# First units' values by whole rows and a GpSimd spread, a new instruction list, and the zero products moved to the front

## The chip, the cores and the metric

The kernel runs on 1 core of a Trainium2 chip. The metric is the device time of one execution in microseconds. The kernel before was timed three times: median 895.59 us (895.14 to 896.82). A further execution was recorded by the hardware profiler.

## What is computed

Attention over q, k, v of shape (8, 8, 576, 64) in float32, followed by a feed-forward stage on the 4608 x 512 result:

```python
scores = 1/sqrt(D) * q @ k^T
mask_plain = (rel >= 0) & (rel < 32)                      # heads 0 to 3
mask_dil   = (rel >= 0) & (rel < 128) & (rel % 4 == 0)    # heads 4 to 7
attn = softmax(where(mask, scores, -1e9))
x = (attn @ v) laid out as (B*S, 512)
h = x @ w_in                                              # 512 x 2048, float64 weights
g = h * tanh(log1p(exp(min(h, 20))))                      # mish
out = g @ w_out                                           # 2048 x 512, float64 weights
```

The weights arrive as 64-bit floats. The host only lays arrays out and back (q and k transposed, dilated heads sorted by residue, the result transposed).

## The kernel before

**Units.** The work is cut into 16 units, a unit being half of one batch entry's sequence (288 tokens). For a unit, `loads` (step ld) fetches q and k, `loads_v` (lv) the values, `scores_of_pair` (sp), `scores` (sc) and `exps` (ex) form the windowed scores and their exponentials, `transpose_p` (tp), `values` (va) and `transpose_x` (tx) give the attention output with features on the partitions, and `ff1` (ff), `gate` (gt) and `ff2` (fo) or, from unit 8 on, `product` (fq) do the feed-forward stage. Step names carry the unit and the head pair: va1.2 is unit 1, pair 2. A step is a Python generator; each time its name stands in the list, it issues its next part.

**Units 0 to 2** are "direct": their scores and values are float32 matmuls without splitting into two halves, and values have a 65th column of ones per head, so that the value product also gives the softmax denominator. `prep` (pr) finds the largest magnitude of a unit's values; the denominators' step on ScalarE (L829) needs the scale that comes out of it.

**Weights.** w_in (4 groups of 512 columns, two halves each, steps 0.g.p) and w_out (1.g.p) come as 64-bit words through four buffers of 1 MB (`w_load`, wl). Each half goes through `w_max` (wm, ScalarE L400 for w_in, GpSimd L398 for w_out), `w_words` (ww: GpSimd L441, then VectorE L443 and L445), a maximum over the group on TensorE and VectorE (`w_scale`, ws: L412 or L415, L419) and `w_split` (wp: ScalarE L452, VectorE L454) into two float16 parts. A buffer is free again after its L454.

**The order** is written out: `ORDER` is a list of some 2250 step names, and every engine and queue executes its instructions in the order in which the list issues them. A queue never overtakes: an instruction that waits holds up all behind it on its engine. SyncE's queue carries every load and store. `=n` behind a name picks a PSUM bank.

**Zero products.** `keep_warm` (kw, L1137 to 1140) issues n matmuls of a zero tile, 128 columns wide, into a PSUM bank; nobody reads them. The list holds 42 ahead of the first scores (kw16, kw16, kw10) and 101 more between unit 0's and unit 2's attention (kw9, kw16, kw16, kw8, kw10; kw8; kw16, kw16; kw2).

**Values of a direct unit** (L494 to L510) are loaded straight into the tile with 65 columns per head, so each row of 1 KB in memory becomes four pieces of 256 B; a unit takes three such transfers for the plain heads (L508) and four for the dilated ones (L510).

## Time and profile before

| | us |
|---|---|
| median of three runs | 895.59 |
| the profiled execution | 897.61 |
| its span, first to last instruction | 895.6 |
| PE (TensorE matmuls) busy | 875.9 (98%) |
| DVE (VectorE) busy | 706.0 (79%) |
| ACT (ScalarE) busy | 621.4 (69%) |
| POOL (GpSimd) busy | 69.9 (8%) |

Times in the rows further down are counted from the span's start. PEld is TensorE's weight load, which overlaps matmuls. SPq is SyncE's DMA issue. The granted clock of TensorE is given as a share of 2.4 GHz: 0.50 is 1.2 GHz. A DMA share is the mean busy share of the core's 16 DMA engines. In brackets behind an instruction stands how long its engine had been idle before it and what ended that.

### The profile page before, as it was taken

To read this page: it belongs to the slowest core of one execution; us is meant where nothing else is said; L and a number is where in the kernel's file an instruction comes from. 1 tells how busy PE (TensorE), PEld (TensorE's weight loads), DVE (VectorE), ACT (ScalarE), POOL (GpSimd) and SP (SyncE) were. 2 spreads that over 40 slices of the span, in tenths; PEclk is the share of its full clock that TensorE was granted. 3 is DMA by queue.
4 is the path that set the end of the run, shared out by engine and by line. 5 is a ranking of instruction groups with operands and counts; after the bars stand their busy time and mean duration, and the time that the engine had idled before them with its cause. 6 is when DMAs were issued, how large, how long until landed. Compare 5 with 4: busy or idle time off the path is not lost.

```text
span 895.6 us, 23819 instructions
## 1 busy us (share of the span) xinstructions
PE 875.9 (98%) x10264; PEld 741.2 (83%) x10266; DVE 706.0 (79%) x1035; ACT 621.4 (69%) x924; POOL 69.9 (8%) x117
## 2 busy tenths in 40 slices
...
PEclk9699999999999999999999999999999999999999
...
GB/s 211 186 272 199 108 142 10 105 29 160 68 106 72 103 87 70 104 149 47 136 102 83 69 47 133 74 113 74 115 69 42 131 79 50 43 35 72 15 28 28
DMA packets 161464, 84.34 MB, mean 94 GB/s; under 512 B 127056, under 2 KB 157264, under 8 KB 161360
## 3 DMA queue, kind: packets, MB, share of 16 engines
...
## 4 chain that ended last, share of the span: by engine, by line
PE 90%; DVE 3%; DMA 2%; POOL 1%; SPq 1%; ACT 1%; issue 1%; DVEq 0%; ACTq 0%; POOLq 0%
PE b L923 39%; PE b L1111 21%; PE b L1062 18%; PE b L672 4%; PE b L821 4%; PE b L815 1%; DVE w L443 1%; POOL w L398 1%; DMA raw<-in_w_out 1%; DMA vn<-in_v 1%; DVE raw L445 1%; DVE w L454 1%; PE b L415 1%; DMA x<-x 0%; PE b L792 0%
## 5 line engine op out<-in xcount | busy, mean ns | idle before, releaser
L923 PE MATMUL b<-x,w 128*128 128x288 f16 x3072 | 390.0, 286 | 1.4 <-ACT den L829 1.1
L923 PEld LDWEIGHTS <-w 128*128 128x128 f16 x3072 | 297.8, 98 | 75.7 <-DVE w L454 1.2
L1111 PE MATMUL b<-g,w 128*128 128x288 f16 x1536 | 198.6, 286 | 0.0
L1111 PEld LDWEIGHTS <-w 128*128 128x128 f16 x1536 | 147.3, 98 | 36.9 <-issue 0.2
L929 ACT ACTIVATE hm<-b,fs 128x576 f32<-128x576 f32 x128 | 92.9, 737 | 73.2 <-PE b L923 68.6
L1062 PE MATMUL b<-g,w 128*128 128x144 f16 x1536 | 101.2, 226 | 0.4 <-DVE y L1081 0.2
L1062 PEld LDWEIGHTS <-w 128*128 128x128 f16 x1536 | 97.6, 98 | 1.6 <-issue 0.6
L1034 ACT ACTIVATE g<-hm,sg 128x1152 f16<-128x1152 f32 (+1 forms) x64 | 71.5, 1127 | 16.9 <-PE b L1062 14.0
L1036 DVE SCALAR_TENSOR_TENSOR g<-hm,sg,g 128x1152 f16<-128x1152 f32 (+1 forms) x64 | 79.8, 1261 | 4.3 <-ACT g L1034 4.2
L743 ACT ACTIVATE sb<-sb,ln_p 96x768 f32<-96x768 f32 (+3 forms) x52 | 46.1, 893 | 10.4 <-DVE sb L704 10.3
L704 DVE TENSOR_TENSOR sb<-sb,nm 96x512 f32<-96x512 f32 (+4 forms) x64 | 49.2, 769 | 2.2
L1081 DVE SCALAR_TENSOR_TENSOR y<-b,fo,y 128x144 f32<-128x144 f32 x48 | 20.6, 475 | 38.2 <-ACT y L1076 23.7
L782 DVE TENSOR_TENSOR p<-sb,p 96x768 f16<-96x768 f32 (+3 forms) x52 | 47.0, 905 | 4.5 <-ACT p L780 4.4
L702 DVE TENSOR_REDUCE nm<-sb 96x4 f32<-96x512 f32 (+4 forms) x64 | 48.8, 763 | 1.8
L1042 DVE TENSOR_TENSOR hm<-hm 128x576 f32<-128x576 f32 x64 | 47.8, 754 | 2.8 <-ACT hm L929 1.8
L1076 ACT ACTIVATE y<-b,fo 128x288 f32<-128x288 f32 x32 | 24.7, 779 | 34.5 <-PE b L1062 34.3
L1013 DVE SCALAR_TENSOR_TENSOR g<-hm,sg,g 128x1152 f16<-128x1152 f32 x32 | 44.8, 1409 | 2.8 <-ACT g L1011 2.8
L836 DVE TENSOR_TENSOR xs<-b,rec 96x384 f32<-96x384 f32 (+1 forms) x64 | 39.7, 621 | 5.8
L780 ACT CAST p<-sb 96x768 f16<-96x768 f32 (+3 forms) x52 | 40.8, 790 | 2.8 <-DMA pT<-p 2.6
L1011 ACT ACTIVATE g<-hm,sg 128x1152 f16<-128x1152 f32 x32 | 39.8, 1249 | 3.6 <-PE b L1111 3.2
L1062 PE MATMUL b<-g,g 128*128 128x144 f16 x576 | 40.3, 226 | 1.1 <-ACT y L1076 1.1
L821 PEld LDWEIGHTS <-pT 128*128 128x128 f16 (+2 forms) x1092 | 39.3, 98 | 1.7
(169 smaller groups left out, 1166.4 us busy)
## 6 DMA issues: line engine op xcount, KB each, us to landing
...
```

The lines of the kernel that those rows point to most:

```text
L702: nc.vector.tensor_reduce(nm[:nq, :, j:j + n], x, axis=AX.X, op=ALU.max, negate=True)
L704: nc.vector.tensor_tensor(blocked(sb, c0, n, w), x, nm[:nq, :, j:j + n].unsqueeze(3).broadcast_to([nq, 2, n, w]), op=ALU.add)
L743: nc.scalar.activation(x, x, AF.Exp, bias=ln_p[:nq])
L782: nc.vector.tensor_tensor(lo, src, hi, op=ALU.subtract)
L821: nc.tensor.matmul(avv[:, h, j], pp[:nk, c:c + P], vv[vi][:nk, j, hh, :], start=(i == 0), stop=(i == 2))
L923: nc.tensor.matmul(ph[:, h, :HT], w1[j][:, c, wi, k * P:(k + 1) * P], x_of(d, xi, c), start=(n == 0), stop=(n == len(seq) - 1))
L929: nc.scalar.activation(d["m"][p][:, half, k0:k0 + 2], ph[:, :, :HT], AF.Mish, scale=d["fs"][:, j:j + 1])
L1034: nc.scalar.activation(hi, src, AF.Identity, scale=sg)
L1036: nc.vector.scalar_tensor_tensor(lo, src, sg, hi, ALU.mult, ALU.subtract)
L1042: nc.vector.tensor_tensor(a, a, b, op=op)
L1062: nc.tensor.matmul(acc[e], left(l, e, p, wi)[:, k * P:(k + 1) * P], right(gi, k), start=(n in opens and p == 0 and q == 0), stop=(last and ...
L1111: nc.tensor.matmul(po[:, :HT], w2[:, e, j, wi, k * P:(k + 1) * P], d["g"][j][:, gi, k, :], start=(j == 0 and n == 0), stop=(j == NCH - 1 a ...
```

## The change

- `loads_v`: all plain blocks of a unit come in one transfer (two for the first half of a batch entry) and all dilated residues in one, by whole rows of 1 KB. For units 0 to 2 they land in a part of w_out's still empty tile `w2` (float32), and a second part of the step copies them with GpSimd into the tile with 65 columns per head. Unit 0's transfers are issued by ScalarE's queue, all others by SyncE's.
- `keep_warm` writes into a fixed strip of 96 columns of the last bank, 96 columns per product. The list holds 56 such products (kw32, kw24) ahead of the first scores and none later.
- `ORDER` is new as a whole. Unit 1's values are loaded before unit 0's and both ahead of the first weights; unit 2's values come before unit 2's q and k.
- `product` takes its three output slices from `po` where they exist; this only allows other orders of the steps.

The code, and of both lists the start (up to the second maximum of w_out) and the last lines:

```diff
@@ -26,6 +26,7 @@
 SPLIT_EXP = 13
 SUM_EXP = 14
 OUT_EXP = 12
+WIDE_MAX = 96
 LOW_SCALE, LOW_BIAS = 0.9375 * 2.0 ** -29, -2.0 ** -5
 TINY = 2.0 ** -40
 EXP_BITS = 0x7F800000
 ORDER = """
-mf cs3 ld0 cs1 xa0 xa1 cs0 kw16=0 kw16=0 kw10=0 sp0.0=0 sp0.1=1 sp0.2=2 lv0 pr0 sp0.3=3 sc0.1 ex0.1 wl0.0.0 lv1 ex0.1
-sc0.3 ex0.3 sc0.2 ex0.2 wl0.0.1 sc0.0 ex0.3 pr0 pr0=1 wl0.3.1 tp0.3=3 wl0.3.0 ld1 pr0 pr1 pr0 ex0.2 tp0.2=2 pr0 tp0.3
-wm0.0.0 ww0.0.0 ex0.0 va0.3=3 ww0.0.1 ww0.0.0 tp0.2 va0.2=1 ex0.0 tp0.0=2 va0.3 va0.2 va0.3 tp0.1=0 va0.2 ww0.3.1
-tx0.3=3 tp0.0 va0.0=2 tx0.2=1 tp0.1 va0.1=0 tx0.3 tx0.3 va0.0 tx0.2 tx0.2 pr1 pr1 ww0.3.0 va0.1 wm0.0.1 wm0.3.1
-ww0.0.0 va0.0 kw9=3 tx0.0=2 tx0.0 kw16=3 kw16=3 kw8=3 tx0.0 tx0.0 va0.1 tx0.1=0 tx0.1 kw10=3 sp1.0=2 wm0.3.0 tx0.1
-ww0.0.1 ww0.3.1 ww0.3.1 ww0.0.1 tx0.3 wm0.3.0 tx0.2 ww0.3.0 ww0.3.0 ww0.3.0 ww0.3.0 ws0.3=3 sp1.2=1 sc1.0 tx0.1
-ws0.0=0 ex1.0 ws0.3 sp1.1=3 sc1.2 wp0.3.1 tp1.0=2 ex1.2 kw8=0 tp1.2=1 tp1.0 wp0.3.1 ws0.0 ld2 tp1.2 sp1.3=2 ww0.3.0
-sc1.3 va1.2=0 wl0.1.0 ww0.1.0 va1.0=1 wp0.0.1 wp0.0.1 sc1.1 wp0.0.0 wl0.2.1 pr1=3 wp0.3.0 ww0.2.1 wp0.0.0 wl0.1.1
-ww0.1.1 ex1.3 ex1.1 kw16=3 kw16=3 tp1.1=2 pr1 wm0.1.0 wp0.3.0 va1.2 tp1.3=3 tp1.1 wl0.2.0 va1.2 va1.0 ww0.1.0 tp1.3
-ff0.6=2 tx1.2=0 va1.0 wm0.2.1 ww0.2.1 va1.1=3 tx1.2 tx1.0=1 ff0.6 lv2 va1.1 cs2 tx1.0 tx1.0 va1.1 va1.3=3 ww0.1.0
-wm0.1.1 ww0.1.1 tx1.2 lv3 ww0.2.0 tx1.0 ws0.1=1 va1.3 va1.3 tx1.3=3 ws0.1 tx1.2 tx1.1=0 ff0.1=1 wm0.2.0 ww0.2.0 tx1.1
-tx1.1 tx1.3 tx1.3 ww0.2.0 kw2=3 ws0.2=0 tx1.3 wp0.1.0 sp2.0=3 ws0.2 ff1.6=0 ff1.6 sc2.0 fs0.0 wp0.2.0 ft wp0.1.0
-wp0.2.0 wl1.2.0 fs0.1 ff0.1 ww0.1.1 ex2.0 fs0.2 fs0.3 ff0.1 fs1 wp0.1.1 ff0.6 wm1.2.0 ff1.1=3 ff1.1 ww1.2.0 ff1.7=1
-ff1.7 ff0.0=2 ww0.2.1 wp0.2.1 pr2 wp0.1.1 ff0.0 wl1.3.1 ff1.7 ff1.6 wp0.2.1 pr2 ff0.0 sp2.3=1 ff0.7=0 ww1.3.1 wl1.2.1
-fs0.4 gt0.0=0 sc2.3 wl1.3.0 gt0.0 wm1.3.1 tp2.0=2 ff0.7 ff1.1 ff1.0=3 ff1.0 tp2.0 ww1.2.1 ex2.3 wm1.2.1 ff0.7 ff1.2=2
-ww1.2.0 ww1.2.0 gt0.3=1 ww1.3.0 ww1.3.1 ff1.4=1 ff1.0 ww1.2.1 ww1.3.1 wm1.3.0 ff1.4 ww1.3.0 ws1.3=0 gt1.0=2 ww1.2.1
-gt1.3=3 ws1.3 wp1.3.1 ws1.2=3 ws1.2 wp1.2.0 wp1.3.1 gt0.3 wl1.0.0 wm1.0.0 wp1.2.1 ff1.2 ff0.3=0 ff0.3 ff1.5=3 ww1.0.0
...
-ga15.1 ga15.1 gq15.1.2=2 fq14.5.1 fq15.0.1 gq15.0.2 gq15.0.3 fq15.3.0 gq15.1.2 fq15.3.1 fq15.1.1 gq15.1.3=3 fq15.3.1
-gq15.1.3 fq15.2.0 fq15.4.0 fq14.6.1 fq15.4.1 fq15.2.1 fq15.4.1 fq15.6.0 fq15.6.1 fq15.4.1 fq15.5.0 fq15.6.1 fq15.6.1
-fq15.5.1 fq15.5.1 fq15.5.1
+cs1 mf cs0 ld0 kw32 kw24 sp0.0=0 lv1 lv1 cs3 xa0 xa1 lv0 lv0 sp0.2=1 sp0.3=2 sp0.1=3 sc0.2 sc0.3 ex0.3 wl0.0.0 wl0.0.1
+ex0.2 wl0.3.0 sc0.0 ww0.0.0 ex0.3 tp0.3=2 sc0.1 ex0.1 ex0.0 ex0.2 tp0.2=1 pr1 tp0.3 pr0 tp0.2 pr1 pr0 pr0=2 wl0.3.1
+pr0 pr0 ex0.0 pr0 ld1 va0.2=1 wm0.0.0 va0.3=2 ww0.0.0 ex0.1 va0.3 va0.3 tp0.0=0 tp0.1=3 va0.2 va0.2 tx0.3=2 ww0.0.1
+tx0.2=1 tp0.0 va0.0=0 wm0.0.1 tx0.3 tx0.3 tp0.1 va0.1=3 ww0.3.0 ww0.0.0 ww0.0.1 va0.0 va0.0 tx0.0=0 pr1 wm0.3.0
+ww0.3.0 tx0.2 tx0.2 va0.1 va0.1 tx0.1=3 tx0.0 tx0.0 ww0.3.0 wm0.3.0 ww0.3.0 tx0.1 tx0.1 ww0.3.0 wm0.3.1 ww0.0.1
+ww0.3.1 tx0.2 sp1.0=1 ww0.3.1 ww0.3.1 tx0.3 tx0.1 sc1.0 ws0.3=2 sp1.2=3 ws0.3 tx0.0 ex1.0 sp1.3=0 tp1.0=2 ws0.0=1
+wp0.3.1 tp1.0 sc1.2 sp1.1=3 ex1.2 tp1.2=2 sc1.3 ex1.3 pr1=0 tp1.2 ws0.0 va1.0=1 wp0.3.1 va1.2=2 sc1.1 tp1.3=3 wp0.0.1
+pr1 wp0.0.1 ex1.1 tp1.1=0 va1.0 lv2 ld2 va1.2 wl0.1.0 tp1.3 ww0.3.0 va1.0 tx1.0=3 va1.3=1 tp1.1 va1.2 tx1.2=0 wp0.3.0
+lv2 wp0.0.0 va1.1=2 wl0.2.1 wp0.3.0 tx1.0 tx1.0 tx1.2 tx1.2 wp0.0.0 ww0.1.0 va1.1 va1.1 va1.3 ww0.2.1 va1.3 tx1.3=2
+wm0.1.0 tx1.1=1 ww0.1.0 tx1.2 ff0.6=0 tx1.0 tx1.1 tx1.1 wl0.1.1 ww0.1.0 ff0.6 tx1.3 ww0.1.1 wl0.2.0 wm0.2.1 wm0.1.1
+tx1.3 tx1.3 ff1.7=3 ww0.2.0 ww0.2.1 ww0.1.1 ws0.1=1 ws0.1 wm0.2.0 wp0.1.0 ww0.2.0 ww0.1.1 ff1.1=2 ff1.1 wp0.1.1
+ws0.2=1 ws0.2 ft ff1.7 lv3 pr2 wp0.1.1 fs1 ff1.0=1 ff1.1 ff1.0 ff1.7 sp2.0=2 wl1.3.0 ww0.2.1 ff1.0 ff0.7=3 ff0.7
+ww0.2.0 wp0.1.0 fs0.0 gt1.0=0 wp0.2.1 wp0.2.1 ww1.3.0 wp0.2.0 ff0.1=1 ff0.1 pr2 wl1.3.1 fs0.1 fs0.2 sc2.0 fs0.3 ff0.6
+sp2.3=0 wp0.2.0 wl1.2.0 sc2.3 wl1.2.1 ff0.7 ff1.6=3 ff0.1 ff0.0=1 ff1.6 wm1.3.0 ww1.3.1 ex2.0 fs0.4 ww1.3.0 gt1.0
+ex2.3 wm1.3.1 ff1.2=2 ff1.2 ww1.3.1 ff0.0 ww1.3.1 ws1.3=0 ff1.6 ff1.5=3 ww1.3.0 ww1.2.1 gt1.3=1 ws1.3 wm1.2.0 gt1.3
+wp1.3.0 ff1.5 gt0.3=2 ff0.0 wp1.3.0 ww1.2.0 gt0.3 ff1.3=0 ff1.5 wm1.2.1 gt0.0=3 pr2 ww1.2.0 ff1.3 ff1.3 ff0.4=1 ff0.4
+wp1.3.1 tp2.3=3 ww1.2.1 wl1.0.0 ff1.2 wp1.3.1 ws1.2=0 ws1.2 gt0.0 wl1.0.1 ww1.2.1 ww1.0.0 ww1.2.0 tp2.3 ff0.2=2 ff0.2
...
+fq15.1.1 fq15.3.0 fq15.3.1 fq14.6.1 fq15.3.1 fq15.2.0 fq15.4.0 gq15.1.3 fq15.4.1 fq15.2.1 fq14.6.1 fq15.4.1 fq15.4.1
+fq15.6.0 fq15.5.0 fq15.6.1 fq15.6.1 fq15.5.1 fq15.5.1 fq15.6.1 fq15.5.1
@@ -493,21 +493,31 @@
         b, half, kd = d["b"], d["half"], d["kd"]
         i0 = 0 if half == 0 else RB - WIN
         if d["direct"]:
-            vn = pool.tile([P, NPB, 4, D + 1], F32, tag="vh", name="vn", bufs=2)
-            vdn = pool.tile([KD, NR, 4, D + 1], F32, tag="vdh", name="vdn", bufs=2)
-            nc.gpsimd.memset(vn[:, :, :, D:], 1.0)
-            nc.gpsimd.memset(vdn[:, :, :, D:], 1.0)
-            d["vh"], d["vdh"] = [vn], [vdn]
+            home = w2[:, u % 2].rearrange("p j i n -> p (j i n)").bitcast(F32)
+            vn, vdn = (home[:, n0:n0 + n * 4 * D].rearrange("p (j h d) -> p j h d", j=n, h=4)
+                       for n0, n in ((0, NPB), (NPB * 4 * D, NR)))
         else:
             vn = pool.tile([P, NPB, 4, D], F32, tag="lD", name="vn")
             vdn = pool.tile([KD, NR, 4, D], F32, tag="lE", name="vdn")
-        vn, vdn = d["vn"], d["vdn"] = vn[:, :, :, :D], vdn[:, :, :, :D]
-        for j in range(NPB):
-
-            r0 = max(half * HT + j * QB - (P - QB), 0)
-            nc.sync.dma_start(vn[:, j], v[b, r0:r0 + P].rearrange("k (h d) -> k h d", h=4))
-        for r in range(NR):
-            nc.sync.dma_start(vdn[:kd, r], vd[b, r, i0:i0 + kd, :].rearrange("k (h d) -> k h d", h=4))
+        d["vn"], d["vdn"] = vn, vdn
+        queue = nc.scalar if u == 0 else nc.sync
+        for j0, n in ((0, NPB),) if half else ((0, 1), (1, NPB - 1)):
+            r0 = max(half * HT + j0 * QB - (P - QB), 0)
+            rows = v[b, r0:r0 + P]
+            src = bass.AP(rows.tensor, rows.offset, [list(rows.ap[0]), [QB * rows.ap[0][0], n], list(rows.ap[1])])
+            queue.dma_start(vn[:, j0:j0 + n].rearrange("k j h d -> k j (h d)"), src)
+        queue.dma_start(vdn[:kd].rearrange("k r h d -> k r (h d)"), vd[b, :, i0:i0 + kd, :].rearrange("r k c -> k r c"))
+        if not d["direct"]:
+            return
+        vh = pool.tile([P, NPB, 4, D + 1], F32, tag="vh", name="vn", bufs=2)
+        vdh = pool.tile([KD, NR, 4, D + 1], F32, tag="vdh", name="vdn", bufs=2)
+        nc.gpsimd.memset(vh[:, :, :, D:], 1.0)
+        nc.gpsimd.memset(vdh[:, :, :, D:], 1.0)
+        d["vh"], d["vdh"] = [vh], [vdh]
+        d["vn"], d["vdn"] = vh[:, :, :, :D], vdh[:, :, :, :D]
+        yield
+        nc.gpsimd.tensor_copy(vh[:, :, :, :D], vn)
+        nc.gpsimd.tensor_copy(vdh[:kd, :, :, :D], vdn[:kd])
 
     def prep(u):
         d = U[u]
@@ -1064,7 +1074,7 @@
         if p == 0:
             return
         fo = d["fo"][:, :1]
-        x, y, z = (d["po"][i][:, :, i * HF:(i + 1) * HF] for i in range(3))
+        x, y, z = (t and t[:, :, i * HF:(i + 1) * HF] for i, t in enumerate(po))
         by = lambda t: t.rearrange("p e (r i) -> p e r i", r=2)
         into = lambda half, t: d["y"][half].rearrange("p e (i r) -> p e r i", r=NR)[:, :, 2 * t:2 * t + 2]
         store = lambda half: nc.sync.dma_start(
@@ -1134,10 +1144,13 @@
     zeros = const.tile([P, P], F16, name="zeros")
     nc.vector.memset(zeros, 0.0)
 
+    spare = banks[-1][:, 1, 512 - WIDE_MAX:]
+    spared = []
+
     def keep_warm(n):
-        warm = take("b", banks)
         for _ in range(n):
-            nc.tensor.matmul(warm[:, 1, 512 - P:], zeros, zeros, start=True, stop=True)
+            nc.tensor.matmul(spare, zeros, zeros[:, :WIDE_MAX], start=not spared, stop=True, skip_group_check=True)
+            spared.append(n)
 
 
     STEPS = {"ld": loads, "lv": loads_v, "pr": prep, "sp": scores_of_pair, "sc": scores, "tp": transpose_p, "va": values, "tx": transpose_x,
```

## Rows read from the trace of the kernel before

**Rows 1.** The profile's page, its first and second part: busy time and share of the span by engine, and the granted clock in 40 slices of 22.4 us, in tenths.

```profile
PE 875.9 (98%) x10264; PEld 741.2 (83%) x10266; DVE 706.0 (79%) x1035; ACT 621.4 (69%) x924; POOL 69.9 (8%) x117
...
PEclk9699999999999999999999999999999999999999
```

**Rows 2.** Busy time of each engine in stretches of 20 us, from the view by windows: length, then PE, PEld, DVE, ACT, POOL busy us (instructions), granted clock, DMA share, GB/s.

```profile
0.00:20.00 20.00, 16.69 (x168) 13.61 (x169) 5.09 (x15) 9.26 (x16) 3.59 (x17) 1.00 0.78 194
...
20.00:40.00 20.00, 17.80 (x156) 15.40 (x157) 16.33 (x27) 11.68 (x26) 4.26 (x4) 0.67 0.69 248
...
40.00:60.00 20.00, 16.55 (x184) 13.21 (x181) 16.43 (x28) 15.05 (x26) 2.94 (x3) 0.91 0.69 227
...
80.00:100.00 20.00, 16.76 (x158) 13.68 (x156) 16.82 (x15) 13.98 (x23) 15.60 (x8) 0.96 0.33 110
```

**Rows 3.** The same view in stretches of 1 us, for the granted clock.

```profile
18.00:19.00 1.00, 0.00 (x0) 0.00 (x0) 0.41 (x1) 1.00 (x3) 0.24 (x1) 1.00 0.50 114
...
20.00:21.00 1.00, 1.00 (x11) 1.00 (x10) 0.98 (x3) 0.35 (x1) 0.00 (x0) 0.50 0.96 299
...
30.00:31.00 1.00, 1.00 (x18) 1.00 (x17) 0.92 (x1) 1.00 (x2) 0.57 (x1) 0.95 1.12 354
...
37.00:38.00 1.00, 0.58 (x1) 0.25 (x2) 1.00 (x2) 0.00 (x0) 0.00 (x0) 0.50 0.00 0
...
44.00:45.00 1.00, 1.00 (x18) 0.85 (x15) 0.39 (x1) 0.12 (x1) 0.00 (x0) 1.00 0.00 0
...
50.00:51.00 1.00, 0.00 (x0) 0.00 (x0) 0.96 (x2) 1.00 (x5) 0.00 (x0) 1.00 0.96 381
```

**Rows 4.** The same view in stretches of 5 us.

```profile
25.00:30.00 5.00, 5.00 (x37) 4.76 (x36) 2.34 (x5) 2.79 (x6) 1.75 (x2) 0.50 1.01 398
...
75.00:80.00 5.00, 5.00 (x44) 3.99 (x42) 4.12 (x4) 4.36 (x8) 2.65 (x1) 1.00 0.93 304
...
95.00:100.00 5.00, 2.35 (x28) 2.36 (x29) 3.93 (x6) 0.80 (x1) 1.33 (x1) 0.84 0.00 0
...
100.00:105.00 5.00, 5.00 (x38) 3.88 (x37) 4.68 (x13) 3.64 (x4) 0.00 (x0) 0.82 0.06 14
```

**Rows 5.** Timeline of SyncE's DMA issues: start us, duration us, engine and line, operation, out<-in, count.

```profile
3.10 2.20 SPq L508 DMA_DIRECT2D vn<-in_v  x3
...
5.34 3.49 SPq L510 DMA_DIRECT2D vdn<-in_vd  x4
...
11.08 1.93 SPq L508 DMA_DIRECT2D vn<-in_v  x3
```

**Rows 6.** Timeline of the first 20 us, the lines that read the values of units 0 and 1 and the first two weight operations: start us, duration us, engine line op out<-in, shape, count, and in brackets the idle time of the engine before it and what ended it.

```profile
8.77 0.84 ACT L527 ACTIVATE w<-vn 128x768 bf16<-128x768 f32 x1 [5.26 <-DMA vn<-in_v]
...
10.86 1.06 ACT L527 ACTIVATE w<-vdn 72x1024 bf16<-72x1024 f32 x1 [1.15 <-DMA vdn<-in_vd]
...
17.13 1.11 POOL L441 TENSOR_SCALAR raw<-raw 128x1024 int32<-128x1024 uint32 x1 [13.95 <-DMA raw<-in_w_in]
...
18.59 0.95 DVE L328 TENSOR_REDUCE m<-vn 128x1 bf16<-128x768 f32 x1 [4.48 <-DMA vn<-in_v]
```

**Rows 7.** The timeline from 18.60 to 32 us: the exponential of unit 0's first pair, value products and transposes on TensorE, and the weight steps of ScalarE and VectorE.

```profile
18.60 0.75 ACT L730 ACTIVATE sb<-b 96x704 f32<-96x704 f32 x1
...
19.75 2.06 PE L815 MATMUL b<-vdn,pp 72*72 72x65 f32 x16 [2.26 <-DVE m L538]
...
20.20 1.22 DVE L443 SCALAR_TENSOR_TENSOR w<-w,raw 128x1024 int32<-128x1024 int32 x1
...
21.61 2.12 PE L792 MATMUL b<-ident,sb 96*128 96x96 f32 x12
...
21.64 0.69 DVE L836 TENSOR_TENSOR xs<-b,rec 72x512 f32<-72x512 f32 x1
...
23.83 0.69 ACT L801 COPY pp<-b 96x192 f32<-96x192 f32 x2 [0.27 <-PE b L792]
...
28.86 2.17 ACT L400 ACTIVATE w<-raw 128x1024 f32<-128x1024 f32 x2
...
30.08 2.82 DVE L443 SCALAR_TENSOR_TENSOR w<-w,raw 128x1024 int32<-128x1024 int32 x2 [0.24 <-ACT w L400]
```

**Rows 8.** The timeline, lines of the zero products (L1140) and the two reductions that waited for such a product.

```profile
1.04 4.66 PE L1140 MATMUL b<-zeros 128*128 128x128 f16 x42 [1.04 <-DVE zeros L1135]
...
45.58 0.69 DVE L419 TENSOR_REDUCE wm<-b 128x1 f32<-128x512 f32 x1 [1.19 <-PE b L1140]
...
51.73 1.95 PE L1140 MATMUL b<-zeros 128*128 128x128 f16 x32
...
53.71 0.16 DVE L538 COPY m<-b 128x1 f32<-128x1 f32 x1 [0.87 <-PE b L1140]
```

**Rows 9.** The timeline from 77 to 98 us, GpSimd's and VectorE's weight steps of w_out and the wait of TensorE for them.

```profile
77.35 2.86 POOL L398 TENSOR_SCALAR w<-raw 128x1024 f32<-128x1024 f32 x1 [13.00 <-DMA raw<-in_w_out]
...
87.33 3.72 POOL L398 TENSOR_SCALAR w<-raw 128x1024 f32<-128x1024 f32 x1
...
92.61 3.72 POOL L398 TENSOR_SCALAR w<-raw 128x1024 f32<-128x1024 f32 x1
...
96.36 1.23 DVE L443 SCALAR_TENSOR_TENSOR w<-w,raw 128x1024 int32<-128x1024 int32 x1 [0.69 <-POOL w L398]
...
97.64 2.99 PE L415 MATMUL b<-w,ones 128*128 128x128 bf16 x32 [3.24 <-DVE w L443]
```

240 lines of the change are left out of this document (120 added, 120 removed).

## Prediction

> **What bounds the kernel now.** I read the page first: PE is busy 98% of the span, and its granted clock is full in all slices but the first few [rows 1]. So whatever the list does after some 105 us, TensorE has work without a gap, and the end comes when its work is through; only what TensorE loses before counts. The view by windows then shows the loss [rows 2]. Idle time is the window less PE busy: 3.31 us in 0 to 20, 2.20 in 20 to 40, 3.45 in 40 to 60, 3.24 in 80 to 100. The clock takes more: (1 - 0.67) x 17.80 = 5.9 us in 20 to 40. And 42 + 101 zero products sit in PE's busy time.
>
> Why TensorE waits is read next from the timeline, on VectorE, the engine that the weights pass through. It stands 4.48 us until unit 1's values land, and its first word step begins at 20.20 [rows 6, 7]: SyncE issues those transfers at 11.08 only, behind seven issues for unit 0 that took 2.20 + 3.49 us [rows 5]. In 25 to 30 us it works 2.34 of 5 us [rows 4]: its next word steps start at 30.08, held by ScalarE's L400 at 28.86 [rows 7], which stands in ScalarE's queue behind the denominators of all four value products of unit 0, and these run at half clock. Between 45 and 54 us two reductions wait 1.19 and 0.87 us for a zero product [rows 8]. Last, TensorE waits 3.24 us at 97.64 for w_out's first maximum (L415): the word step on VectorE at 96.36 came after GpSimd's L398 at 92.61 [rows 9], the last of eight operations that the old list gives GpSimd before it.
>
> **The change, part by part.** I follow the same points in the new list.
>
> *Values.* SyncE now issues unit 1's values in two transfers right behind unit 0's q and k, at 3.1 us; unit 0's go by ScalarE, which has nothing else to do until its first exponential. By shape the bytes are 1152 KB of q and k, 816 KB for unit 1, 672 KB for unit 0, 2.70 MB together. Rows of 1 KB are what w_out's loads move too, 304 GB/s in 75 to 80 us [rows 4]: 8.9 us, from 2 us on, so both are there at about 10.9. Then GpSimd copies 768 + 1024 elements per unit, unit 1 first. The page of before has no such copy. The nearest row is L441 beside it in time, 1.11 us for 1024 elements [rows 6], which makes 1.94 us a unit; the far bound is L398 under contention, 3.72 for 1024 [rows 9], 6.5 us a unit. Nothing is gained below 1.94 that I can name. I take L441's. Unit 0's copies end at 10.9 + 3.9 = 14.8. Behind them on ScalarE: two sums of magnitudes 0.84 + 1.06, a copy 0.69, an exponential 0.75, and half of L400's 2.17 [rows 6, 7], 4.4 us with little between: first word step at about 19.6 instead of 20.20, gain 0.6. At the far bound GpSimd would end 9 us later and the step would come at 28: a loss of 8, less what is gained below because the weights are there earlier.
>
> *ScalarE's order.* The second L400 moves in front of va0.0's denominator, behind the first transposes' copy only. VectorE then does one word step (1.22), two normalisations (0.69 each, plus their reciprocals), two more word steps, and comes to va0.0 at about 25. What is late there is TensorE: from 18.2 us on it has va0.2, va0.3, tp0.0 with tp0.1, two small transposes and va0.0 before it. At half clock that is 3 x 2.06 + 2.12 + about 1.4 (two transposes, a third of L792's row each, my estimate) = 9.7 us [rows 7], until 27.9; at full clock about 4.9, and VectorE wouldn't wait. At half clock it is at 28.4 where the old one was at 30.08, with one word step more and two normalisations less behind it, some 0.6 us of work: 1.1 us earlier. At full clock it is 4.2 earlier. Up to the scores of unit 1 the half-clock case gives 0.6 of it back, since va0.1 is 2.06 us late too. I carry 0.5 us here and keep 4.2 as the other end.
>
> *Zero products.* The 56 in front have 56 x 96 = 5376 columns, as many as 42 x 128, so their 4.66 us [rows 8] should stay; if each cost what a 128-wide one costs (4.66 / 42 = 0.111), they'd take 6.2 and the first scores be 1.5 us late, hidden up to about 2 us because the values come at 10.9. The 101 others go. Two waits go with them, 1.19 + 0.87 = 2.06 us on VectorE's queue. What is late next is the clock. Before, it fell to 0.50 by 20 us after TensorE had nothing in 18 to 19, and again at 37; it was back near 30, just as zeros ran, and at 44 without them [rows 3]. I charge 1.0 us for unit 1's values at half clock for part of the way, so 1.06 remain; nearest evidence is the recovery by 44.
>
> The Trainium skill, "TensorE: Matmul & The Clock Gate", section "HAM oscillation — how this bites in real kernels", says that gaps in which the engine waits let the clock fall to half, so that each burst after a gap starts slow. Our trace agrees for two gaps (0.50 at 20 and 37 us) but shows full clock in 50 to 51 us with PE empty [rows 3], with 32 zeros behind it [rows 8]. By the rule the removed zeros are the cover that kept unit 1 warm; that result is a rival below.
>
> *Unit 2's values and the buffers.* Three issues instead of seven, ahead of unit 2's q and k, into room that is free. Their GpSimd copies (1.94 us, at the far bound 6.5) fall between 25 and 50 us, where GpSimd works 4.26 us of 20 and 2.94 of the next 20 [rows 2]. I cost them at nothing; if VectorE holds them up, w_in's second half starts up to 4 us late. The later units' fewer issues and the guard in `product` cost nothing, as SyncE's queue is not on the path there.
>
> *w_out.* The new list gives GpSimd only the two halves of group 3 before that group's maximum: four operations instead of eight. The four of group 2, priced at 2.86 + 3.72 [rows 9] and twice 1.11 [rows 6], are 8.8 us that go behind. TensorE reaches the maximum after 18 half steps of ff1, one fewer than before, and about 2 us earlier than at 94.4. By the lists VectorE has two word steps, a split and a maximum more to do, less unit 2's first scores, before the first half of w_in's group 1 is split (about 3.5 us), though another split that frees a buffer comes first, so the loads of w_out come about as early as now. With 8.8 - 2 - 1.5 in hand the 3.24 us should go whole, and with them the half clock behind: (1 - 0.84) x 2.35 + (1 - 0.82) x 5.00 = 1.3 us [rows 4]. The next wait is group 2's maximum, six half steps (9 us) later; its four operations take 8.8, so it is just in time. I take 4.5 and keep 0 as the other end.
>
> *Rest and tail.* TensorE is full; small waits there can come and go, 1 us either way. At the end the second to last store moves behind one more product; I take 0, bounded by 1 us.
>
> **Sum.** 0.5 + 1.06 + 4.5 = 6.1 us less. On the profiled execution, 897.61 (span 895.6), that is 891.5; the median of the runs is 2.02 lower, so 895.59 - 6.1 = **889.5 us**.
>
> **Rivals.**
> 1. *Full clock throughout.* If TensorE's denser start keeps the clock up after 20 us, the 4.2 us of the second part come in place of 0.5: 885.8. For it: TensorE is busy 16.69 of the first 20 us and at full clock there [rows 2]; against: a pause for unit 0's scale remains at about 17 us. Chance 0.13.
> 2. *The stall only moves.* Group 2's maximum, or w_in's second half, now ends a wait as long as the old one; the gain is the first parts' 1.5 or less: 894.1 to 895.6. For it: VectorE's total work is the same and it is near full from 30 to 100 us [rows 2]. Against: eight operations become four. Chance 0.17.
> 3. *Slower: the clock stays at half through unit 1.* TensorE's work in 40 to 60 us is 16.55 us at a mean clock of 0.91, 15.1 at full clock, less 1.95 of zeros: 13.1 at full and 26.2 at half [rows 2, 8], which is 9.7 above what was busy. It decides as soon as the clock is not back by about 45 us, since VectorE then waits on each value product. 889.5 + 9.7 = 899.2. Against: it came back at 44 before with the same scores and maxima. By the rule quoted above this would be the outcome, and the trace bears it out in two gaps of three. Chance 0.17.
> 4. *The change doesn't do what it says:* values come no earlier, because copies cost the far bound or both queues share engines that were 0.9 busy. The first step comes 5 us later than I said and about 4 us reach the end: 893.5. Chance 0.10.
>
> **Numbers.** My forecast has 0.43. Its own range is 886.5 to 892.5 (1 us of small waits, 1.3 of the clock, 0.7 of the copies). No change can be told within 0.2%, 893.8 to 897.4. The range is 885 to 897: it leaves out most of the slower rival and a corner of the first. Faster: 0.43 + 0.13, 0.05 of the second and 0.06 of the fourth, 0.67. Same: 0.11 of the second, 0.04 of the fourth and 0.01 of the third, 0.16. Slower: 0.16 of the third and 0.01 of the second, 0.17.
>
> **What would show it.** First L443 near 19.6 us; VectorE's wait in 25 to 30 us moved to va0.0's normalisation; no reduction waiting on L1140; L415 of group 3 without a wait above 0.5 us; PE idle in 80 to 100 us under 0.5. Wrong: granted clock 0.50 beyond 45 us, GpSimd copies above 3 us, or a wait of over 2 us on a maximum of w_out or w_in's second half.

## The result, and the profile after

Nine runs of the changed kernel have a median of 902.23 us (899.76 to 908.22), nine of the kernel before 896.82 (893.45 to 899.89). The ratio is 1.0077, 95% interval 1.0054 to 1.0099: the change makes the kernel slower, by 0.8%. I had predicted 889.5, in a range that ended at 897. The profiled execution took 906.41 us, span 904.6; it lies 4.2 us above the median of its kernel, that of the kernel before 0.8 above, so the 9.0 us between the two spans overstate the 5.4 between the medians.

The page of the changed kernel, parts 1 to 3: busy time, the granted clock in 40 slices, and two of the DMA queues (q1 is SyncE's, q10 ScalarE's) with packets, MB and share.

```profile
PE 878.3 (97%) x10177; PEld 741.8 (82%) x10179; DVE 700.7 (77%) x1035; ACT 615.4 (68%) x920; POOL 76.5 (8%) x123
...
PEclk9579998999999999999999999999999999999999
...
q1 hardware_dynamic: 153228, 82.14, 37.4%
...
q10 hardware_dynamic: 716, 0.69, 0.3%
```

TensorE has the work that it had (875.9 us before, [rows 1]); the 9 us of span are waits and clock. The windows say where, with the columns of [rows 2]:

```profile
0.00:20.00 20.00, 14.69 (x160) 11.83 (x160) 5.41 (x11) 5.09 (x10) 5.17 (x19) 0.99 0.95 302
20.00:40.00 20.00, 14.18 (x89) 12.72 (x90) 11.20 (x24) 12.33 (x23) 10.46 (x10) 0.50 0.54 175
40.00:60.00 20.00, 16.82 (x146) 12.35 (x147) 17.62 (x32) 14.26 (x31) 1.53 (x2) 0.76 0.38 116
80.00:100.00 20.00, 20.00 (x188) 15.99 (x186) 18.75 (x18) 17.45 (x33) 11.09 (x6) 1.00 0.65 211
120.00:140.00 20.00, 16.53 (x173) 13.97 (x172) 15.36 (x28) 14.72 (x31) 12.56 (x6) 0.97 0.56 174
```

In 20 to 40 us TensorE is busy 14.18 us where it was 17.80, all of it at half clock (0.50; before 0.67), and VectorE 11.20 where it was 16.33. 80 to 100 us has no gap any more, as forecast; 3.47 us are missing in 120 to 140 instead. The timeline from 4 to 26 us, in order of time, engines mixed, shows why the front is late:

```profile
4.19 11.79 SPq L378 DMA_DIRECT2D raw<-in_w_in  x8
...
4.59 1.27 ACTq L508 DMA_DIRECT2D w<-in_v  x2
...
6.04 0.57 ACTq L509 DMA_DIRECT2D w<-in_vd  x1
...
10.72 1.04 POOL L520 COPY vdn<-w 104x1024 f32<-104x1024 f32 x1 [1.42 <-DMA w<-in_vd]
...
15.75 0.82 POOL L519 COPY vn<-w 128x768 f32<-128x768 f32 x1 [3.89 <-DMA w<-in_v]
...
20.99 1.04 POOL L520 COPY vdn<-w 72x1024 f32<-72x1024 f32 x1 [4.41 <-DMA w<-in_vd]
...
22.11 5.79 POOL L441 TENSOR_SCALAR raw<-raw 128x1024 int32<-128x1024 uint32 x5
...
23.24 0.16 DVE L544 TENSOR_TENSOR ms<-ms 72x1 f32<-72x1 f32 x1 [9.74 <-ACT w L537]
...
23.45 0.37 PE L344 MATMUL b<-ident,ms 128*1 128x128 f32 x1 [7.72 <-DVE ms L544]
...
25.57 1.37 DVE L443 SCALAR_TENSOR_TENSOR w<-w,raw 128x1024 int32<-128x1024 int32 x1
```

Read it from the bottom. The first word step L443 comes at 25.57 (before 20.20, [rows 7]). VectorE had stood 9.74 us until the sum of unit 0's magnitudes (L537), TensorE 7.72 us behind that. ScalarE had waited for GpSimd's copies, and the copies for data: unit 0's plain heads are there at 15.75, its dilated ones at 20.99, though ScalarE had issued them by 6.6. Beside them run SyncE's eight weight loads, issued from 4.19 on. Unit 1's copies, whose data went by SyncE ahead of the weights, cost 0.82 and 1.04 us, 1.86 together where I had taken 1.94. GpSimd's word steps L441 stand behind the copies and start at 22.11 (before 17.13, [rows 6]). The first first-layer product follows at 65.96, where it was 55.74.

### The profile page after: what moved, and what is told of

It reads as the page before. It is cut to its first block, busy times and chain, and to the rows that moved or that the text cites. A ratio compares the mean times of both kernels' runs of the same rounds, so it can differ in the third digit from the quotient of the medians.

```text
span 904.6 us, 23543 instructions
## 1 busy us (share of the span) xinstructions
PE 878.3 (97%) x10177; PEld 741.8 (82%) x10179; DVE 700.7 (77%) x1035; ACT 615.4 (68%) x920; POOL 76.5 (8%) x123
## 5 line engine op out<-in xcount | busy, mean ns | idle before, releaser
L939 ACT ACTIVATE hm<-b,fs 128x576 f32<-128x576 f32 x128 | 92.3, 737 | 78.1 <-PE b L933 63.1
L1023 DVE SCALAR_TENSOR_TENSOR g<-hm,sg,g 128x1152 f16<-128x1152 f32 x32 | 46.9, 1474 | 4.9 <-ACT g L1021 4.9
L862 ACT CAST x<-xs 96x384 f16<-96x384 f32 (+1 forms) x52 | 29.1, 559 | 24.7 <-DMA x<-x 13.2
L864 DVE TENSOR_TENSOR x<-xs,x 96x384 f16<-96x384 f32 (+1 forms) x52 | 32.0, 616 | 17.6 <-ACT x L862 17.6
L846 DVE TENSOR_TENSOR xs<-b,rec 72x512 f32<-72x512 f32 (+1 forms) x64 | 39.7, 620 | 5.7
L616 POOL MEMSET vh<- 128x12 f16 x26 | 4.2, 166 | 457.9 <-ACT vh L566 395.8
```

The costliest lines, as they stand in the source:

```text
L939: nc.scalar.activation(d["m"][p][:, half, k0:k0 + 2], ph[:, :, :HT], AF.Mish, scale=d["fs"][:, j:j + 1])
L1023: nc.vector.scalar_tensor_tensor(g[:, 1], m, sg, g[:, 0], ALU.mult, ALU.subtract)
```

## The experiments

Theory A: unit 0's values, on a queue of their own, share the DMA engines with 4 MB of weights, and all that follows is late. Theory B: the loss is the clock, which no zeros hold up. Theory C: the new list loses at w_out's first maxima what it gains. Ratios are to the kernel before in the same job, where its median was 896.2 to 897.0, with 95% intervals; they are not quotients of the medians in the table. "ff1" is the start of the first first-layer product in the profiled run, "last max" that of the last group's maximum (L415) that TensorE waits for, with its wait: w_out's group 3 in the old list, group 1 in the new one. These two come from one profiled execution each, which lies above the median of its kernel by 4.2 us (changed), 4.1 (e1), 3.8 (e8) or 1.4 to 2.5 (e2, e3, e5, e7, e11), and within 0.9 of it in the others: a difference of a microsecond or two in them is not one in the medians.

| kernel | list | median us | ratio | ff1 | last max (wait) |
|---|---|---|---|---|---|
| before | old | 896.82 | 1 | 55.74 | 97.64 (3.24) |
| changed | new | 902.23 | 1.0077 (1.0054 to 1.0099) | 65.96 | 140.11 (3.58) |
| e1 sync queue | new | 893.28 | 0.9962 (0.9939 to 0.9985) | 57.99 | 131.29 (2.44) |
| e2 rows only | old | 899.81 | 1.0038 (1.0014 to 1.0062) | 51.53 | 99.33 (5.13) |
| e3 no zeros | old | 899.28 | 1.0011 (0.9989 to 1.0033) | 55.87 | 100.45 (5.09) |
| e4 zeros in wait | new | 899.78 | 1.0029 (1.0005 to 1.0053) | 60.60 | 134.16 (2.43) |
| e5 list only | new | 897.37 | 1.0003 (0.9982 to 1.0025) | 60.40 | 133.37 (2.45) |
| e6 unit 0 first | new | 893.55 | 0.9948 (0.9927 to 0.9968) | 54.24 | 127.07 (2.40) |
| e7 weights behind | new | 895.61 | 0.9979 (0.9959 to 1.0000) | 57.34 | 130.65 (2.38) |
| e8 sync, zeros | new | 893.16 | 0.9949 (0.9924 to 0.9974) | 55.39 | 130.53 (2.45) |
| e9 max on ScalarE | new | 889.13 | 0.9930 (0.9904 to 0.9956) | 53.72 | 123.89 (0.78) |
| e10 rows late | old | 902.10 | 1.0062 (1.0038 to 1.0087) | 50.95 | 99.21 (9.86) |
| e11 = e9 with e8's zeros | new | 892.07 | 0.9953 (0.9934 to 0.9973) | 55.55 | 128.76 (0.78) |
| e12 = e9 again | new | 889.63 | 0.9924 (0.9900 to 0.9949) | 54.19 | 125.48 (0.78) |

**e1, unit 0's values on SyncE's queue.**

```diff
-        queue = nc.scalar if u == 0 else nc.sync
+        queue = nc.sync
```

> The changed kernel with one edit: unit 0's values are issued by SyncE, behind unit 1's and ahead of the weights, and not by ScalarE. Theory A (unit 0's 0.69 MB shares the engines with 4 MB of weights on the other queue and so lands at 15.7 and 21.0 us): GpSimd's copies of unit 0 begin by 13 us in place of 15.75 and 20.99, TensorE's gap of 7.72 us ahead of L344 falls below 2, VectorE's first word step L443 comes at 19 to 21 in place of 25.57, the first first-layer product at 58 to 61 in place of 65.96, and the time is 893 to 898. Theory B (the clock, which has no zeros to hold it): the landing moves, but the clock stays at 0.50 from about 20 to 46, the time gains under 2 us and stays at 900 or more. Theory C (the new list): the wait of 3.58 us on ws1.1's maximum at 140 stays as it is, and of the 5 us gained in front under 2 reach the end.

The timeline of e1:

```profile
6.28 9.51 SPq L378 DMA_DIRECT2D raw<-in_w_in  x8
...
14.23 0.82 POOL L519 COPY vn<-w 128x768 f32<-128x768 f32 x1
...
15.49 1.04 POOL L520 COPY vdn<-w 72x1024 f32<-72x1024 f32 x1 [0.43 <-DMA w<-in_vd]
...
17.95 0.27 PE L344 MATMUL b<-ident,ms 128*1 128x128 f32 x1 [2.04 <-DVE ms L544]
...
19.99 1.22 DVE L443 SCALAR_TENSOR_TENSOR w<-w,raw 128x1024 int32<-128x1024 int32 x1 [0.20 <-ACT w L400]
```

One word in the source takes the whole loss back, and more: 1.0077 becomes 0.9962. The copies come 1.5 and 5.5 us earlier (at 14.23 behind unit 1's copies, not "by 13"), the wait ahead of L344 is 2.04 in place of 7.72, L443 stands at 19.99, ff1 at 57.99. The clock is still 0.50 from 20 to 38 us, so B alone isn't it. The span is 9.0 us shorter and the last maximum 8.8 us earlier: what the front gains reaches the end, against C.

**e7, the same from the other side: ScalarE's queue kept, the weights issued later.**

```diff
+        if u == 0:
+            held = pool.tile([P, 2], F32, name="held", bufs=1)
+            nc.sync.dma_start(held[:1, :1], vdn[:1, NR - 1, 3, D - 1:])
+            nc.sync.dma_start(held[:1, 1:], vn[:1, NPB - 1, 3, D - 1:])
```

> The changed kernel with unit 0's values still on ScalarE's queue, and two four-byte loads put on SyncE behind its values, which read the last word of unit 0's values, so that SyncE issues no weight before those have landed. Theory A: without the weights beside them unit 0's values land by 11.5 (10.9 was my estimate), the copies L519 and L520 begin by 12 in place of 15.75 and 20.99, TensorE's gap ahead of L344 is under 2.5 us, the weights come 5 to 8 us later than they did, and the time is 893 to 900. If ScalarE's queue is slow by itself, the copies still begin behind 15 us and the time is 902 or more.

The timeline of e7 (unit 1's copies, SyncE's held load L512, the first weights, unit 0's copies, L344), and two windows of it:

```profile
12.40 0.82 POOL L523 COPY vn<-w 128x768 f32<-128x768 f32 x1 [9.31 <-DMA w<-in_v]
...
13.68 0.73 SPq L512 DMA_DIRECT2D held<-w  x1
...
14.62 1.04 POOL L524 COPY vdn<-w 104x1024 f32<-104x1024 f32 x1 [1.40 <-DMA w<-in_vd]
...
15.16 4.02 SPq L378 DMA_DIRECT2D raw<-in_w_in  x8
...
15.69 0.82 POOL L523 COPY vn<-w 128x768 f32<-128x768 f32 x1
...
16.45 1.04 POOL L524 COPY vdn<-w 72x1024 f32<-72x1024 f32 x1
...
18.96 0.27 PE L344 MATMUL b<-ident,ms 128*1 128x128 f32 x1 [1.25 <-DVE ms L548]
```

```profile
8.00:11.00 3.00, 1.89 (x35) 1.45 (x36) 0.75 (x1) 0.00 (x0) 0.00 (x0) 1.00 0.84 216
11.00:14.00 3.00, 3.00 (x22) 1.80 (x22) 2.99 (x6) 0.65 (x1) 0.82 (x1) 1.00 0.21 54
```

Little but the weights' start was moved (they come 11 us later, at 15.16 and not at 4.19; ScalarE's issues come 1.6 us earlier), and 0.9979 stands against 1.0077. Unit 0's copies no longer wait for data: they follow unit 1's without a gap. But unit 1's own data are later here (copies at 12.40 and 14.62, in the changed kernel at 8.48 and 10.72), so unit 0's first copy begins at 15.69, behind 15, which I had written down as the sign of the rival. The rest speaks against the rival: the time isn't 902 or more, the wait ahead of L344 is 1.25 in place of 7.72, and from ScalarE's issue of unit 0's dilated part to its landing it is 4.64 to 13.68, 9.0 us, where the copy that waits for it starts 9.8 us behind the issue in e1 on SyncE's queue (5.72 to 15.49) and 15.0 in the changed kernel (6.04 to 20.99). So it isn't ScalarE's queue by itself that is slow. What differs is the bytes moved up to the last landing: by the view of the DMA engines 6.4 MB in the changed kernel (landed by 20.99), 4.0 in e1 (15.49), 2.7 in e7 (13.68), which are the 2.70 of the prediction and nothing beyond. My number for the landing (11.5) was too early here too: SyncE got past the wait on the dilated part at 13.68, with the engines at 216 GB/s in 8 to 11 us and nearly idle in 11 to 14 (share 0.21, 54 GB/s).

**e4, zeros in TensorE's gap** (150 of 96 columns ahead of L344; queue as in the changed kernel). The diff adds one entry to the list, and a bank of their own for zeros with a place.

```diff
-tp0.3 pr0 tp0.2 pr1 pr0 pr0=2
+tp0.3 pr0 tp0.2 pr1 pr0 kw150=2 pr0=2
```

> The changed kernel, queues and list as they are, with 150 zero products of 96 columns (6 us at 40 ns each) put into TensorE's gap ahead of unit 0's transposition L344. Theory A: the values land as late as before, VectorE and GpSimd wait as long, the first first-layer product moves by less than 2 us from 65.96, and the time stays at 900 to 903. Theory B: the granted clock is 1.00 until about 25 and again earlier than 46, the time falls to 898 or less.

One window of e4 (the changed kernel has 0.50 there):

```profile
22.00:24.00 2.00, 1.36 (x15) 1.15 (x16) 1.00 (x7) 2.00 (x4) 1.84 (x3) 1.00 1.00 369
```

Both theories were partly right. The data were about as late (16.47 and 19.81 us), but the clock was 1.00 from 16 to 34 us and back by 42, and ff1 came 5.4 us earlier, which A had not allowed; 1.2 of them are the landing (L344 at 22.27 in place of 23.45). The time, 899.78, is a hair below A's 900 to 903 and not B's 898. So once TensorE has been made to wait, the clock costs more in front, some 4 us by this one pair of traces; 902.23 to 899.78 is what the medians show of it. Late data and half clock are one loss in series, not two theories.

**e8, the same idea where nothing waits long** (e1 with 40 zeros in the remaining wait).

```diff
+        queue = nc.sync
-tp0.3 pr0 tp0.2 pr1 pr0 pr0=2
+tp0.3 pr0 tp0.2 pr1 pr0 kw40=2 pr0=2
```

> The first experiment's kernel (unit 0 on SyncE) with 40 zero products of 96 columns in TensorE's wait ahead of L344. If landing and clock are two separate prices: the clock stays 1.00 from 17 to beyond 25 us where it was 0.50, and the time is 890 to 892 against 893.28. If the front is bound by VectorE and GpSimd once the values are there, the clock rises and the time stays within 1 us of 893.28.

The windows of e8, for the granted clock:

```profile
20.00:22.00 2.00, 1.43 (x20) 1.26 (x19) 1.23 (x5) 1.69 (x5) 1.78 (x3) 1.00 1.04 409
28.00:30.00 2.00, 0.49 (x2) 0.28 (x2) 2.00 (x3) 2.00 (x3) 0.00 (x0) 0.81 0.91 279
30.00:32.00 2.00, 2.00 (x14) 1.25 (x12) 1.97 (x2) 0.91 (x3) 1.93 (x2) 0.50 0.08 32
```

The clock is full to 28 us, 0.50 behind that, ff1 is 2.6 us earlier than in e1, and the last maximum (130.53 against 131.29) and the time (893.16 against 893.28) are the same. So zeros as a means to hold the clock buy nothing here. What the clock alone would be worth no run separates, since the zeros have a price of their own: unit 0's values landed earlier in this execution (see the end), its sum was ready at 15.53, and the 40 zeros from 15.33 on, 1.86 us, kept L344 until 17.03.

**e3, the zeros behind the first scores taken out of the old list.**

```diff
-kw9=3 ... kw16=3 kw16=3 kw8=3 ... kw10=3 ... kw8=0 ... kw16=3 kw16=3 ... kw2=3
```

> The kernel before without its 101 zero products behind the first scores; nothing else is changed. Theory B: the granted clock is 0.50 for most of 20 to 57 us (before: 20 to 30 and 37 to 43.6), and the time is 900 to 904, most of the change's loss. Theory A: the two waits on zeros (1.19 and 0.87 us) go, the clock is low for a few microseconds more, and the time is 895 to 899.

The clock is 0.50 from 23 to 43 us, longer than with the zeros, though not to 57 as B had it, and the ratio 1.0011 can't be told from 1 (899.28, between the times of the two theories). The 101 zeros held the clock for a part of that time and bought nothing that could be measured, nor did their removal bring the 1.06 us that I had booked; the interval leaves room for 1 us gained and for 3 lost.

**e2 and e10, the loads alone, in the old list.** e2 replaces `loads_v` by the new one, all on SyncE, with lv0, lv1 and lv2 doubled in the list; e10 moves the second lv2 ahead of the first pr2.

```diff
-ff0.6 lv2 va1.1
+ff0.6 lv2 lv2 va1.1
```

```diff
-ff0.6 lv2 lv2 va1.1
+ff0.6 lv2 va1.1
-wp0.2.1 pr2 wp0.1.1
+wp0.2.1 lv2 pr2 wp0.1.1
```

> The kernel before, with its old list and all its zero products, and only the loads changed: whole rows and GpSimd's copies for units 0 to 2, all on SyncE's queue, the copies as a second step right behind each load. By my prediction's own terms: the values' issues fall from 14 to 5 on SyncE, the weights are issued earlier, unit 0's copies cost 0.8 to 1.1 us each, first L443 within 1 us of 20.20, time 893 to 898 against 896.82. If the copies or the whole rows as such are what costs, the time is 900 or more.

> The second experiment's kernel (old list, new loads on SyncE) with unit 2's GpSimd copies moved from right behind their loads to right before unit 2's maxima. The theory: that kernel was 6.4 us ahead of the kernel before at L335 (45.27 against 51.70) and lost it because GpSimd stood 5.62 us at unit 2's values, with w_in's last word step behind them. Then GpSimd's last word step of w_in starts before 58 in place of 62.59, SyncE issues w_out at 67 to 70 in place of 71.81, and the time is 893 to 897 against 899.81. The rival: the loss sits further behind, in w_out's first group on GpSimd, whose wait was 5.13 us at 99.33: it stays above 4 us and the time at 898 or more.

The timeline of e2, from GpSimd's copies for unit 2 to the last maximum:

```profile
60.27 0.82 POOL L519 COPY vn<-w 128x768 f32<-128x768 f32 x1 [5.62 <-DMA w<-in_v]
...
62.59 1.09 POOL L441 TENSOR_SCALAR raw<-raw 128x1024 int32<-128x1024 uint32 x1
...
94.34 3.68 POOL L398 TENSOR_SCALAR w<-raw 128x1024 f32<-128x1024 f32 x1
...
99.33 3.60 PE L415 MATMUL b<-w,ones 128*128 128x128 bf16 x32 [5.13 <-DVE w L443]
```

The same of e10, with GpSimd's first operation on w_out and its wait for a later piece:

```profile
56.91 2.39 POOL L441 TENSOR_SCALAR raw<-raw 128x1024 int32<-128x1024 uint32 x1 [1.27 <-DMA raw<-in_w_in]
...
72.29 2.87 POOL L398 TENSOR_SCALAR w<-raw 128x1024 f32<-128x1024 f32 x1 [12.99 <-DMA raw<-in_w_out]
...
86.15 2.04 POOL L441 TENSOR_SCALAR raw<-raw 128x1024 int32<-128x1024 uint32 x1 [1.96 <-DMA raw<-in_w_out]
...
99.21 3.59 PE L415 MATMUL b<-w,ones 128*128 128x128 bf16 x32 [9.86 <-DVE w L443]
```

The new loads do what they should (ff1 4.2 us earlier), and the kernel is slower, 1.0038, 899.81 where I had expected 893 to 898. My theory for e10 was that unit 2's copies, 5.62 us in wait at 60.27, hold up w_in's last word step behind them. e10 refutes it as the cause: the step starts at 56.91 and w_out is issued at 67.17, 4.6 us earlier than in e2, and yet the wait for group 3's maximum grows from 5.13 to 9.86 us and the time is 902.10, as the rival had it. In the old list TensorE comes to that maximum earlier and finds it no earlier. GpSimd begins w_out 5.4 us earlier than in e2 (72.29, 77.70) and then stands 1.96 us at 86.15 for w_out's data; its last L398 starts at 94.21, as in e2 (94.34; before 92.61). So what holds the maximum is w_out's later pieces; why these came no earlier was not settled. That is rival 2 of the prediction, in the list that I hadn't expected it in.

**e5, the list alone**: the changed kernel with the old `loads_v`.

```diff
-        queue = nc.scalar if u == 0 else nc.sync
...
+        for j in range(NPB):
...
+            nc.sync.dma_start(vn[:, j], v[b, r0:r0 + P].rearrange("k (h d) -> k h d", h=4))
```

> The changed kernel's list and its 56 zeros in front, with the loads of the kernel before: values straight into the 65-column tiles by 14 strided loads on SyncE, unit 1's ahead of unit 0's and both ahead of the weights, nothing copied by GpSimd. If my prediction's largest term is right (the new list takes the wait of 3.24 us on ws1.3 out, 4.5 with its clock), the time is 890 to 895 and a wait on ws1.1 near 131 to 140 of 2.4 to 3.6 us is what it gives back. If the new list only pays with the new loads, the first word step L443 comes behind 24 us, because unit 0's values are now last of the 14, and the time is 898 to 904.

1.0003: no change, a time in neither of my two cases. The wait on group 3 is gone and the one on group 1 (2.45 us) is there, as the first case had it. List alone 1.0003, rows alone 1.0038, both together on one queue 0.9962: only the two together are faster than the kernel before.

**e6, e9, e11, e12: what is left.** e6 exchanges lv0 and lv1 in e1's list, e9 adds a condition in `w_max`, e11 zeros to e9:

```diff
-lv1 lv1 cs3 xa0 xa1 lv0 lv0
+lv0 lv0 cs3 xa0 xa1 lv1 lv1
```

```diff
-            if (k, g) in BY_POOL:
+            if (k, g) in BY_POOL and (k, g, p) != (1, 1, 1):
```

> The first experiment's kernel (unit 0 on SyncE) with the two value steps of units 0 and 1 exchanged in the list, so that unit 0's values are issued and copied first. Theory A (what counts is when unit 0's values land and are copied): GpSimd's copies of unit 0 at about 8 to 10.6 and 13 in place of 14.23 and 15.49, the wait of 2.04 us ahead of L344 goes, the first first-layer product comes 1 to 2 us earlier, time 890 to 893 against 893.28. The rival: VectorE's maxima of unit 1 (L328) now wait for unit 1's copies at 14 to 16 us and hold the head of VectorE's queue, so that L443 stays at 20 and the time at 893 to 896.

> The kernel of the unit-0-first experiment with one piece of w_out more off GpSimd: the magnitudes of its second group's second half (L398, 2.83 us on GpSimd at 121.77) are taken by ScalarE with L400. The theory: in the new list the start of L415 for ws1.1 sets the end (span less its start is 764.5 within 1 us in seven kernels so far), and GpSimd's four operations ahead of it, 9.6 us from 115.97, are what it waits for. Then the wait of 2.40 us there falls below 0.5, and the time to 890 to 892 against 893.55. The rival: ScalarE's operation waits for the weights at the head of its queue and holds back unit 2's exponentials, and the time stays at 893 or above.

```diff
-tp0.2 pr1 pr0 pr0=2
+tp0.2 pr1 pr0 kw40=2 pr0=2
```

> The ninth experiment's kernel with the 40 zero products of the eighth in front of L344. If the clock of the first 40 us is worth anything once the wait on ws1.1 is gone, the time is 1 to 2 us below the ninth's; if not, within 0.5 us of it.

> The ninth experiment's kernel once more, since it has six runs only and the eleventh, which adds zeros to it, did not repeat its time. If the piece moved to ScalarE is worth what the ninth showed, the median is 888 to 891 and TensorE's wait on ws1.1's maximum stays below 1 us; if the ninth was a lucky draw, 892 to 894.

The timeline of e6, GpSimd ahead of the last maximum, and TensorE:

```profile
115.97 3.40 POOL L398 TENSOR_SCALAR w<-raw 128x1024 f32<-128x1024 f32 x1 [6.13 <-DMA raw<-in_w_out]
...
119.45 2.24 POOL L441 TENSOR_SCALAR raw<-raw 128x1024 int32<-128x1024 uint32 x1
...
121.77 2.83 POOL L398 TENSOR_SCALAR w<-raw 128x1024 f32<-128x1024 f32 x1
...
124.67 1.09 POOL L441 TENSOR_SCALAR raw<-raw 128x1024 int32<-128x1024 uint32 x1
...
127.07 1.01 PE L415 MATMUL b<-w,ones 128*128 128x128 bf16 x8 [2.40 <-DVE w L443]
```

The same of e9, with ScalarE's operation that replaces one of the four:

```profile
112.50 1.13 ACT L400 ACTIVATE w<-raw 128x1024 f32<-128x1024 f32 x1
...
114.58 3.25 POOL L398 TENSOR_SCALAR w<-raw 128x1024 f32<-128x1024 f32 x1 [6.30 <-DMA raw<-in_w_out]
...
117.91 3.45 POOL L441 TENSOR_SCALAR raw<-raw 128x1024 int32<-128x1024 uint32 x2
...
123.89 0.61 PE L415 MATMUL b<-w,ones 128*128 128x128 bf16 x8 [0.78 <-DVE w L443]
```

The clock behind that wait, a window of e6 and one of e12:

```profile
120.00:130.00 10.00, 7.61 (x66) 6.21 (x64) 7.42 (x18) 6.02 (x14) 7.19 (x5) 0.85 0.17 47
```

```profile
125.00:130.00 5.00, 4.52 (x49) 3.91 (x48) 4.76 (x12) 4.05 (x6) 0.00 (x0) 1.00 0.00 0
```

And TensorE's front in e11, with L344 of e9 for comparison:

```profile
15.64 1.86 PE L1153 MATMUL b<-zeros 128*128 128x96 f16 x40
...
17.34 0.27 PE L344 MATMUL b<-ident,ms 128*1 128x128 f32 x1
```

```profile
15.47 0.27 PE L344 MATMUL b<-ident,ms 128*1 128x128 f32 x1
```

In e6 the wait ahead of L344 goes, ff1 comes 3.8 us earlier than in e1 and the last maximum 4.2, and yet the medians are the same (893.55, 893.28; 890 to 893 was expected). The traces can't say where a gain would have gone, since e1's profiled execution lies 4.1 us above its median and e6's 0.2. With one magnitude of 2.83 us moved from GpSimd to ScalarE (1.13 us there) the wait on group 1 falls from 2.40 to 0.78 and the median to 889.13, six runs, and again 889.63, six runs, in e12. The intervals of the ratios of e6 and these two overlap, but the twelve runs of e9 and e12 lie in 887.6 to 891.5 us and those of e6 in 889.9 to 895.7. That is the best kernel of the study, 0.7% below the kernel before. The wait is only 1.6 us of what was gained. Behind it e6's clock falls to 0.50 (127 to 130 us), in e9 and e12 it stays at 1.00; busy time times the missing share of the clock makes that another 1.7 us, my estimate from windows of 1 us. The rest isn't placed. e11 was to show whether the clock of the front helps there: 892.07, three microseconds more than e9. It doesn't answer that, because its 40 zeros stand where nothing is waited for: L344 comes at 17.34 in place of 15.47, and ff1 1.8 us later. Its TensorE also waits 1.03 us at 110.21 for ScalarE's L939, which e9's doesn't; why, was not settled.

## Why the prediction was wrong, point by point

**Values: this step failed.** "8.9 us, from 2 us on, so both are there at about 10.9" adds up the bytes of q, k and the values alone and puts the weights beside them at nothing. I had written myself that unit 0's go by ScalarE, so nothing put the weights behind them; SyncE issued them at 4.19, ahead of unit 0's. From 5 to 21 us the changed kernel moves 297 to 404 GB/s (means of 3 us), at shares above 1.0: some 5.5 MB, of which 0.69 are unit 0's. The landing was 15.75 and 20.99, and the first word step 25.57 where I had 19.6. Two errors are in the 10.9. The weights beside the values are the larger: 7.3 us, from 13.68 with nothing beside them (e7) to 20.99. The rate is the smaller: 2.8 us, since even alone the 2.7 MB were there at 13.68 and not at 10.9, at 309 GB/s in 2 to 8 us and only 142 behind that. (By the view of the DMA engines unit 1's values are 800 KB, not 816; it changes nothing.)

With the queue put right (e1) the first word step comes at 19.99, 0.4 from the forecast. That is luck: the data were there at 15.5 and not at 10.9, with some of the weights moved before them even there, but only the last copy (1.04 us) stood behind the landing and not 3.9, and ScalarE's first sum had already run by then.

The Trainium skill, "DMA: Bandwidth & Descriptors", section "Queues, rings and completion order", says that an engine takes turns between the queues that have work, packet by packet. The trace agrees that the small queue isn't served first: it got about an eighth of the bytes while both had work. The profile shows 716 packets for its 0.69 MB, 0.96 KB each, beside weight rows of 4 KB by shape; if these were the pieces that take turns, even turns would give it a fifth, by estimate. No run here shows whether they are, or varied their size, so the eighth stays unexplained.

**ScalarE's order.** I had booked 0.5 at half clock and kept 4.2 for full clock, which is also rival 1. It didn't come about: the clock was 0.50 from 20 us on. e8 has the full clock only to 28 us and with 40 zeros in it; 2.6 us at ff1, and none of it reaches the end.

**Zero products.** The 56 in front took what I said (4.66 us; the first scores begin at 6.06, before 6.22), and the rest was neutral (e3), not 1.06 us of gain. In the changed kernel the clock is 0.50 from 20 to 46 us behind 7.72 us without work, and in e4, where zeros fill that gap, 1.00 to 34 us. The rule of the Trainium skill that the prediction quotes ("TensorE: Matmul & The Clock Gate", section "HAM oscillation — how this bites in real kernels") is that gaps in which the engine waits let the clock fall; the trace agrees in both. The low clock outlasts the gap, though: in 25 to 35 us of the changed kernel TensorE is busy without a break, and the clock is 0.50 to 46 us. Rival 3 was right that the half clock would last beyond 45 us, but not that missing zeros alone make it: with the wait cut to 2.04 us (e1) the clock still falls, at 19 us, and is back at 39, and with zeros in the long wait (e4) it holds to 34 and is back by 42. Both the wait for data and the missing zeros are in it, and no run parts what each costs.

**w_out.** "The 3.24 us should go whole" was right, and "the next wait is group 2's maximum" was wrong: groups 2 and 0 pass, and group 1, the last, waits 3.58 us in the changed kernel and 2.4 in e1 and e4 to e8. I had stopped two groups early. The stall moved and cost as much as before: 3.24 us and 1.7 of clock at group 3 in the kernel before, 2.44 and 1.6 at group 1 in e1 (the clock's part an estimate, as in e6). That is rival 2's case with another group. So the 4.5 us were no gain by themselves (e5: 1.0003). Span less the start of that L415 is 761.9 to 764.9 us in all ten profiles of the new list, and at the low end of it (to 763.1) in e9, e11 and e12, whose clock stays up: behind it everything is fixed within 3 us, and GpSimd's chain ahead of it, not the first stall, is what the list has to clear. e9 does that, and arrives near where I had put the change, at 889, by another road than mine.

**What the two steps make.** The forecast was 12.7 us too low. The queue is about 9 of it by the medians (902.23 to 893.28 in e1) and 10 by the ratios (1.0077 to 0.9962), the stall at group 1 about 4 by the medians (893.55 in e6 to 889.13 and 889.63) and 2 by the ratios (0.9948 to 0.9930 and 0.9924). That the two add up to the miss is in part chance: the 0.5 and the 1.06 us in the sum were not seen in any run, and e9 and e12 have units 0 and 1 exchanged as well.

**Unit 2's values, tail.** Costed at nothing, and nothing shows in the new list: in e1 w_in's second half is issued at 46.27 (before 46.36) in spite of 5.3 us of GpSimd copies for unit 2. A loss or gain at the tail can't be told apart.

**Rivals.** What happened is rival 4 with rival 3's half clock behind it and, at w_out, rival 2's moved stall. Rival 4 named the reason ("both queues share engines that were 0.9 busy") and got 0.10 and a price of 893.5, because it still held the 4.5 us of w_out and let the loss be 5 us once. The first word step came 6.0 us later than I said (25.57, 19.6), and ff1 10.2 us later than in the kernel before, since half clock and GpSimd's blocked word steps added to it. My range ended at 897 because I had left out most of rival 3, which I gave 0.17 and 899.2.
